# Decode attention on one core: heads 1 to 14 as a loop on the chip over standing buffers

## The chip, the cores and the metric

The kernel runs on one core of a Trainium2 chip. The core has five engines that run their own instruction streams and wait for one another by semaphores: TensorE (PE in the profile; its weight loads are listed as PEld), VectorE (DVE), ScalarE (ACT), GpSimd (POOL) and SyncE (SP). Sixteen DMA engines move data between HBM and the core's memory SBUF; a DMA is issued by an engine's queue, here nearly always SP's. TensorE writes its results to PSUM. The metric is the device time of one execution in microseconds; lower is better. The time before is 1314.99 us, the median of 3 runs (1314.83 to 1315.04).

## What is computed

One decode step of a transformer block in float32: a batch of 2, one new token each of width 448, attention with 16 heads of width 256 over a cache of 8192 keys and values, then a gated feed-forward part.

```python
B, Sq, D = 2, 1, 448
H, Sk, Dh = 16, 8192, 256
def _A_ref(x, k_cache, v_cache, wq, wo):
    q = (x @ wq).reshape(B, Sq, H, Dh).transpose(0, 2, 1, 3)
    scores = jnp.einsum("bhqd,bhkd->bhqk", q, k_cache) * (Dh ** -0.5)
    p = _softmax(scores, axis=-1)
    o = jnp.einsum("bhqk,bhkd->bhqd", p, v_cache)
    return o.transpose(0, 2, 1, 3).reshape(B, Sq, H * Dh) @ wo
h = x + _A_ref(_layernorm(x), k_cache, v_cache, wq, wo)
g, u = _layernorm(h) @ w_gate, _layernorm(h) @ w_up
h2 = h + (g * u) @ w_down
```

The two caches are 268 MB each, so nearly all that is read is cache, and each byte of it is used once.

## The kernel before

The program is written out in full by Python loops; the chip runs it straight through, without a branch.

**Steps.** The work goes in 32 steps, `n = 2 * head + batch`, and a 33rd that finishes (line 306). In step n the scores of (head, batch) number n are formed, and the values of number n - 1 are mixed. A step loads two key tiles and two value tiles, each 128 partitions x 32 keys x 256 numbers, 32 KB on each partition and 4096 KB in all. The order on SP's queue is k0(n), v0(n - 1), k1(n), v1(n - 1) (`load_cache`, line 160). Behind the first v stands a weight tile in three of four steps: `wo` for one head (448 KB, lines 316 to 319) or `wq` for a pair of heads (896 KB, line 320).

**Buffers.** All cache tiles come from one pool, `ring`, with 4 buffers that are handed out in turn. A tile's load waits until the tile four loads earlier has been used up. In the first step only two tiles are loaded, so the second step's k0 and v0 get the third and the fourth buffer. The feed-forward weights (lines 346 to 360) go through the same ring behind the last value tile. The small tiles (scores `s`, `p`, `m`, `rl`, `o_sb` and so on) come from pools of 2.

**One step on the engines.** `scores` (line 232) runs on DVE, in four parts per step: a product of half a key tile with the query, broadcast over the keys (line 239, into the one buffer `prod`), and the sum over the 256 numbers of a key (line 242). A key tile is free for its next load when the product of its second half is done. `top` (line 246) takes the maximum on DVE and transposes it on PE; `softmax` (line 253) is called in the next step behind the first part of the scores: maximum on DVE (line 255), a broadcast on PE (line 257), the exponential on ACT (line 262), the row sum on PE (line 266). `norm` (line 268) takes the reciprocal on DVE behind the second part. `mix` (line 272) multiplies p with a value tile on PE, and `mixed` (line 283) folds the result and, behind batch 1, multiplies it with `wo` into `acc_ps`, which adds up over all heads.

**Queries.** `first_queries` (line 191) and `queries` (line 206) compute q for two heads and both batches at a time on PE; for pair hp + 1 they stand between the two halves of `mix` in the last step of pair hp (line 336). ACT copies them to SBUF.

**The end.** Behind the last step `h_sb` is x plus `acc_ps` (line 389), then come the norm, the gate, the up and the down projections and the output.

The program is laid down in the order in which it is written (`manual_schedule`); each engine runs its own instructions in that order, and waits are put in by the framework where one tile is used by several engines.

Of the kernel before, what the change touches and what calls it, by code (L numbers as in the profile page):

```python
# [24 lines left out]
RING = 4  # L25
WQ, WO = 3 * 2 * DH + DH, 2 * D
# [17 lines left out]
def tile_decode_block(  # L44
# [27 lines left out]
    ps_q = ctx.enter_context(tc.tile_pool(name="ps_q", bufs=2, space=bass.MemoryType.PSUM))  # L72
    ps_s = ctx.enter_context(tc.tile_pool(name="ps_s", bufs=2, space=bass.MemoryType.PSUM))
    ps_1 = ctx.enter_context(tc.tile_pool(name="ps_1", bufs=1, space=bass.MemoryType.PSUM))
# [24 lines left out]
    o_ps = [ps_1.tile([P, 2 * DH], F32, name=f"o_ps{i}") for i in range(2)]  # L99
    for t in o_ps:  # L100
        nc.vector.memset(t, 0.0)  # L101
    acc_ps = ps_1.tile([B, D], F32, name="acc_ps")
    y_ps = ps_1.tile([P, YW], F32, name="y_ps")
    nc.vector.memset(y_ps, 0.0)

# [11 lines left out]
    def center(h, tag):  # L117

        mean = ps_s.tile([P, B], F32, tag="sm", name=f"mean_{tag}")
# [18 lines left out]
    def transposed(src, tag):  # L138
        ps = ps_s.tile([P, DC, B], F32, tag="sm", name=f"T_ps_{tag}")
# [7 lines left out]
    def load_wq(hp):  # L147
        t = wpool.tile([P, WQ], F32, tag="wq", name=f"wq_{hp}")
        nc.sync.dma_start(t, wq[hp])
        return t  # L150

    wo_t = {}

    def load_wo(h):

        if h % 2 == 0:
            wo_t[h // 2] = wpool.tile([P, 2, WO], F32, tag="wo", name=f"wo_{h // 2}")
        nc.sync.dma_start(wo_t[h // 2][:, h % 2, :], wo[h])

    def load_cache(src, b, h, c, name, parts=(JC,)):  # L160
        t = ring.tile([P, JC, DH], F32, tag="ring", name=f"{name}_{h}_{b}_{c}")
        n = P * JC
        keys = src[b, h, c * n : (c + 1) * n].rearrange("(p j) d -> p j d", p=P)
        at = 0
        for k in parts:
            nc.sync.dma_start(t[:, at : at + k, :], keys[:, at : at + k, :])
            at += k
        return t

    w_now = load_wq(0)  # L170
# [6 lines left out]
    var = ps_s.tile([P, B], F32, tag="sm", name="var_x")  # L177
# [13 lines left out]
    def first_queries(w):  # L191

        got = [qpool.tile([P, 2, DH], F32, tag="q", name=f"q_0_{b}") for b in range(B)]
        for k in range(2):
            for b in range(B):
                ps = ps_q.tile([P, DH], F32, tag="q", name=f"q_ps_0_{k}_{b}")
                for c in range(DC):
                    at = c * 2 * DH + (k * DH if c < DC - 1 else 0)
                    nc.tensor.matmul(  # L199
                        ps, xb[:, c + (k if c == DC - 1 else 0), b, :], w[:, at : at + DH],  # L200
                        start=(c == 0), stop=(c == DC - 1),
                    )
                nc.scalar.activation(got[b][:, k, :], ps, AF.Copy)
        return got

    def queries(hp, w):

        got = []
        for b in range(B):
            ps = ps_q.tile([P, 2 * DH], F32, tag="q", name=f"q_ps_{hp}_{b}")  # L210
            for c in range(DC - 1):
                nc.tensor.matmul(  # L212
                    ps, xb[:, c, b, :], w[:, c * 2 * DH : (c + 1) * 2 * DH],
                    start=(c == 0), stop=False,
                )
            for k in range(2):
                nc.tensor.matmul(  # L217
                    ps[:, k * DH : (k + 1) * DH], xb[:, DC - 1 + k, b, :],
                    w[:, 3 * 2 * DH : WQ], start=False, stop=(k == 1),
                )  # L220
            q = qpool.tile([P, 2, DH], F32, tag="q", name=f"q_{hp}_{b}")
            nc.scalar.activation(q.rearrange("p h d -> p (h d)"), ps, AF.Copy)  # L222
            got.append(q)
        return got


    NQ = H * B
    w_t, q_t = {0: w_now}, {0: first_queries(w_now)}
    s_t, p_t, rl_t, l_t, mT_t, oT_t = {}, {}, {}, {}, {}, {}
    HC = JC // 2  # L230

    def scores(i, kt, part):

        h, b = divmod(i, B)
        if part == 0:
            s_t[i] = work.tile([P, NJ], F32, tag="s", name=f"s_{i}")
        c, k = divmod(part, 2)
        q = q_t[h // 2][b][:, h % 2, :]
        nc.vector.tensor_mul(  # L239
            prod, kt[c][:, k * HC : (k + 1) * HC, :], q[:, None, :].to_broadcast([P, HC, DH])  # L240
        )
        nc.vector.tensor_reduce(  # L242
            s_t[i][:, part * HC : (part + 1) * HC], prod, axis=AX.X, op=ALU.add
        )

    def top(i):

        m = work.tile([P, 1], F32, tag="m", name=f"m_{i}")
        nc.vector.tensor_reduce(m, s_t[i], axis=AX.X, op=ALU.max)  # L249
        mT_t[i] = ps_s.tile([1, P], F32, tag="sm", name=f"mT_{i}")  # L250
        nc.tensor.transpose(mT_t[i], m, ident)  # L251

    def softmax(i):
        nm = work.tile([1, 1], F32, tag="nm", name=f"nm_{i}")
        nc.vector.tensor_reduce(nm, mT_t[i], axis=AX.X, op=ALU.max, negate=True)  # L255
        nb_ps = ps_s.tile([P, 1], F32, tag="sm", name=f"nb_ps_{i}")
        nc.tensor.matmul(nb_ps, row, nm, start=True, stop=True)  # L257
        nb = work.tile([P, 1], F32, tag="nb", name=f"nb_{i}")
        nc.scalar.activation(nb, nb_ps, AF.Copy)  # L259
        p_t[i] = work.tile([P, NJ], F32, tag="p", name=f"p_{i}")  # L260
        lsum = work.tile([P, 1], F32, tag="lsum", name=f"lsum_{i}")
        nc.scalar.activation(  # L262
            p_t[i], s_t[i], AF.Exp, bias=nb, scale=DH**-0.5, accum_out=lsum
        )
        l_t[i] = ps_s.tile([P, 1], F32, tag="sm", name=f"l_ps_{i}")
        nc.tensor.matmul(l_t[i], ones, lsum, start=True, stop=True)  # L266

    def norm(i):
        rl_t[i] = work.tile([P, 1], F32, tag="rl", name=f"rl_{i}")
        nc.vector.reciprocal(rl_t[i], l_t[i])  # L270

    def mix(i, vt, c):

        o, p = o_ps[i % 2], p_t[i]
        for t in range(c * JC // 2, (c + 1) * JC // 2):
# [3 lines left out]
                o[g : g + 2, :], p[:, 2 * t : 2 * t + 2], vt[c][:, j : j + 2, :],  # L279
# [3 lines left out]
    def mixed(i):  # L283

        h, b = divmod(i, B)
        o_sb = work.tile([P, 2 * DH], F32, tag="o_sb", name=f"o_sb_{i}")
        nc.scalar.activation(o_sb, o_ps[i % 2], AF.Copy)  # L287
        oT_ps = ps_s.tile([P, 2], F32, tag="sm", name=f"oT_ps_{i}")
# [6 lines left out]
        if b == 0:  # L295
            oT_t[h] = work.tile([P, 2, B], F32, tag="oT", name=f"oT_{h}")
        nc.scalar.activation(oT_t[h][:, :, b], oT_ps, AF.Copy, scale=rl_t[i])  # L297
        if b == B - 1:
            w = wo_t[h // 2][:, h % 2, :]
            for c in range(2):  # L300
                nc.tensor.matmul(  # L301
                    acc_ps, oT_t[h][:, c, :], w[:, c * D : (c + 1) * D],
                    start=(h == 0 and c == 0), stop=(h == H - 1 and c == 1),
                )

    for n in range(NQ + 1):
        kt, vt = [], []
        hp, at = divmod(n, 2 * B)
        for c in range(NCH):
            if n < NQ:  # L310
                parts = FIRST if n == 0 and c == 0 else (JC,)
                kt.append(load_cache(k_cache, n % B, n // B, c, "k", parts))
            if n > 0:
                parts = LAST if n == NQ and c == NCH - 1 else (JC,)
                vt.append(load_cache(v_cache, (n - 1) % B, (n - 1) // B, c, "v", parts))
            if c == 0 and at == 1:
                load_wo(2 * hp)
            if c == 0 and at == 3 and hp + 1 < H // 2:
                load_wo(2 * hp + 1)
            if c == 0 and at == 2 and hp + 1 < H // 2:  # L320
                w_t[hp + 1] = load_wq(hp + 1)
        if n == NQ:
            load_wo(H - 1)
        if n < NQ:
            scores(n, kt, 0)
        if n > 0:
            softmax(n - 1)
# [175 lines left out]
```

## Time and profile before

| what | value |
|---|---|
| median of 3 runs | 1314.99 us |
| the profiled execution's own time | 1314.9 us |
| its span, first to last instruction | 1313.1 us |
| read from HBM | 561.19 MB, 427 GB/s over the span |
| mean granted TensorE clock | 0.653 |
| instructions | 6974 |

The page gives the busy time of each engine, then the span in 40 slices with a digit for the busy share in tenths, then the DMA queues and the largest groups of instructions. A row of a group is: line, engine, operation, written <- read, shapes, count, then busy time and mean time of one in ns, then idle time ahead of it and what ended it. A row of the timeline is: start in us, length in us, engine, line, operation, and in brackets the idle time ahead of it with the engine and line that ended it. A row of DMA issues ends with the size of one in KB and the median time in us from issue to landing. The two operations on which DVE spends nearly all its time, a product and a sum over half a key tile, have these rows:

```profile
L239 DVE TENSOR_TENSOR prod<-k,q 128x4096 f32<-128x4096 f32 x128 | 565.7, 4420 | 115.6 <-DMA k<-in_A_k_cache_dram 110.7
L242 DVE TENSOR_REDUCE s<-prod 128x16 f32<-128x4096 f32 x128 | 565.8, 4420 | 6.0
```

### The profile page before, as it was taken

The numbers are of one execution on the slowest core, as the hardware profiler recorded it, in microseconds if no ns is written. First come the engines' busy times: TensorE is split into PE (matmuls) and PEld (weight loads), VectorE is DVE, ScalarE is ACT, GpSimd is POOL, SyncE is SP. The second block draws the span as 40 slices with busy tenths as digits, with TensorE's granted clock in tenths as the row PEclk, the third lists the DMA queues.
The fourth block names the chain that finished last, engine by engine and source line by source line (L and its number), as shares of the span: only waits on it lengthen the run. The fifth ranks groups of instructions, "written<-read, shape, count | busy, mean of one in ns | idle before, by whom it ended". The sixth has DMA issues, their size and how long they took to land.

```text
span 1313.1 us, 6974 instructions
## 1 busy us (share of the span) xinstructions
PE 569.9 (43%) x2936; PEld 173.4 (13%) x2936; DVE 1153.3 (88%) x395; ACT 60.7 (5%) x183; POOL 1.2 (0%) x8
## 2 busy tenths in 40 slices
PE   3224553354432743426433453524525246254357
PEld 2011110111010210102110021101101002011013
DVE  7999999898998899888998889988998989989971
ACT  1000000000000000000000000000000000000000
POOL 0000000000000000000000000000000000000000
PEclk8556766657765666657666567666676667565668
DMA  9999999999999999999999999999999999999997
GB/s 408 430 430 433 430 432 429 428 433 433 431 428 434 430 431 426 435 429 432 431 431 431 434 429 431 430 425 434 430 431 431 433 428 435 431 430 431 431 424 336
DMA packets 23091, 561.64 MB, mean 428 GB/s; under 512 B 2578, under 2 KB 2580, under 8 KB 5908
## 3 DMA queue, kind: packets, MB, share of 16 engines
q1 hardware_dynamic: 23048, 561.20, 99.6%
q8 instruction: 23, 0.38, 0.1%
q14 instruction: 8, 0.07, 0.0%
q10 hardware_dynamic: 12, 0.01, 0.0%
HBM read 561.19 MB, written 0.00 MB: 427 GB/s over the span
## 4 chain that ended last, share of the span: by engine, by line
DMA 79%; PE 14%; DVE 5%; issue 1%; ACT 0%; POOLq 0%; SPq 0%; POOL 0%
DMA v<-in_A_v_cache_dram 77%; PE o_ps L278 13%; DVE prod L239 3%; DMA wu_t<-in_B_w_up_dram 2%; DVE s L242 2%; PE q_ps L199 0%; PE u_ps L379 0%; PE y_ps L438 0%; DVE o_ps L101 0%; PE hm_ps L431 0%; PE oT_ps L291 0%; ACT o_sb L287 0%; PE mean_x L120 0%; DVE xb L134 0%; PE var_x L178 0%
## 5 line engine op out<-in xcount | busy, mean ns | idle before, releaser
L239 DVE TENSOR_TENSOR prod<-k,q 128x4096 f32<-128x4096 f32 x128 | 565.7, 4420 | 115.6 <-DMA k<-in_A_k_cache_dram 110.7
L242 DVE TENSOR_REDUCE s<-prod 128x16 f32<-128x4096 f32 x128 | 565.8, 4420 | 6.0
L278 PE MATMUL o_ps<-v,p 128*2 128x512 f32 x2048 | 371.3, 891 | 338.1 <-DMA v<-in_A_v_cache_dram 338.1
L278 PEld LDWEIGHTS o_ps<-v,p 128*2 128x2 f32 x2048 | 59.2, 109 | 613.6 <-DMA v<-in_A_v_cache_dram 367.3
L257 PE MATMUL nb_ps<-nm,row 1*128 1x1 f32 x64 | 17.9, 347 | 280.0 <-DVE nm L255 280.0
L257 PEld LDWEIGHTS nb_ps<-nm,row 1*128 1x128 f32 x64 | 15.7, 303 | 287.2 <-issue 158.7
L287 ACT ACTIVATE o_sb<-o_ps 128x512 f32<-128x512 f32 x32 | 19.1, 597 | 679.2 <-PE o_ps L278 679.2
L301 PE MATMUL acc_ps<-wo,oT 128*2 128x448 f32 x64 | 43.9, 834 | 5.6 <-ACT oT L297 5.6
L291 PE MATMUL oT_ps<-sel,o_sb 128*128 128x1 f32 x256 | 33.7, 253 | 23.2 <-ACT o_sb L287 23.2
L212 PE MATMUL q_ps<-wq,xb 128*128 128x512 f32 x84 | 39.1, 601 | 0.0
L291 PEld LDWEIGHTS oT_ps<-sel,o_sb 128*128 128x128 f32 x256 | 31.0, 191 | 55.9 <-ACT o_sb L287 55.9
L251 PE MATMUL mT<-ident,m 128*1 128x128 f32 x32 | 10.2, 318 | 61.2 <-DVE m L249 60.9
L266 PE MATMUL l_ps<-lsum,ones 128*128 128x1 f32 x64 | 18.7, 362 | 23.5 <-ACT p L262 23.5
L259 ACT ACTIVATE nb<-nb_ps 128x1 f32<-128x1 f32 x32 | 5.5, 171 | 406.8 <-PE nb_ps L257 406.8
L266 PEld LDWEIGHTS l_ps<-lsum,ones 128*128 128x128 f32 x64 | 16.0, 310 | 26.2 <-ACT p L262 26.2
L212 PEld LDWEIGHTS q_ps<-wq,xb 128*128 128x128 f32 x84 | 15.4, 190 | 20.6 <-issue 20.3
L217 PE MATMUL q_ps<-wq,xb 128*128 128x256 f32 x56 | 14.4, 379 | 0.0
L251 PEld LDWEIGHTS mT<-ident,m 128*1 128x1 f32 x32 | 2.5, 79 | 84.7 <-issue 50.0
L389 DVE TENSOR_TENSOR h_sb<-x_sb,acc_ps 2x448 f32<-2x448 f32 x1 | 0.6, 609 | 13.8 <-PE acc_ps L301 13.8
L222 ACT ACTIVATE q<-q_ps 128x512 f32<-128x512 f32 x14 | 8.4, 597 | 92.1 <-PE q_ps L217 92.1
L217 PEld LDWEIGHTS q_ps<-wq,xb 128*128 128x128 f32 x56 | 10.6, 190 | 7.4 <-issue 6.7
L262 ACT ACTIVATE p<-s,nb 128x64 f32<-128x64 f32 x32 | 11.1, 348 | 1.0
(79 smaller groups left out, 101.8 us busy)
## 6 DMA issues: line engine op xcount, KB each, us to landing
k<-in_A_k_cache_dram SPq DMA_DIRECT2D x63, 4096.0 KB, 26.5
v<-in_A_v_cache_dram SPq DMA_DIRECT2D x63, 4096.0 KB, 33.2
wq<-in_wq_dram SPq DMA_DIRECT2D x8, 896.0 KB, 34.6
wo<-in_wo_dram SPq DMA_DIRECT2D x16, 448.0 KB, 33.5
k<-in_A_k_cache_dram SPq DMA_DIRECT2D x2, 2048.0 KB, 13.5
wg_t<-in_B_w_gate_dram SPq DMA_DIRECT2D x1, 3136.0 KB, 24.5
wu_t<-in_B_w_up_dram SPq DMA_DIRECT2D x1, 3136.0 KB, 30.4
v<-in_A_v_cache_dram SPq DMA_DIRECT2D x1, 2048.0 KB
```

What stands on the lines that cost most here:

```text
L212: nc.tensor.matmul(ps, xb[:, c, b, :], w[:, c * 2 * DH : (c + 1) * 2 * DH], start=(c == 0), stop=False,)
L217: nc.tensor.matmul(ps[:, k * DH : (k + 1) * DH], xb[:, DC - 1 + k, b, :], w[:, 3 * 2 * DH : WQ], start=False, stop=(k == 1),)
L239: nc.vector.tensor_mul(prod, kt[c][:, k * HC : (k + 1) * HC, :], q[:, None, :].to_broadcast([P, HC, DH]))
L242: nc.vector.tensor_reduce(s_t[i][:, part * HC : (part + 1) * HC], prod, axis=AX.X, op=ALU.add)
L251: nc.tensor.transpose(mT_t[i], m, ident)
L257: nc.tensor.matmul(nb_ps, row, nm, start=True, stop=True)
L262: nc.scalar.activation(p_t[i], s_t[i], AF.Exp, bias=nb, scale=DH**-0.5, accum_out=lsum)
L266: nc.tensor.matmul(l_t[i], ones, lsum, start=True, stop=True)
L278: nc.tensor.matmul(o[g : g + 2, :], p[:, 2 * t : 2 * t + 2], vt[c][:, j : j + 2, :], start=(t < 4), stop=(t >= NJ // 2 - 4),)
L287: nc.scalar.activation(o_sb, o_ps[i % 2], AF.Copy)
L291: nc.tensor.matmul(oT_ps[:, c : c + 1], o_sb[:, (2 * k + c) * P : (2 * k + c + 1) * P], sel[:, k : k + 1], start=(k == 0), stop=(k == 1),)
L301: nc.tensor.matmul(acc_ps, oT_t[h][:, c, :], w[:, c * D : (c + 1) * D], start=(h == 0 and c == 0), stop=(h == H - 1 and c == 1),)
```

## The change

Head 0 and head 15 stay written out; heads 1 to 14 become the body of a loop that the chip runs 14 times, with the head's number in a register (`For_i`). The loop's semaphores are not reset between turns: they only rise, and a wait in the body compares with a register that is stepped in each turn. No engine gets a hint of the branch at the loop's end (`HINT = ()`); PE's body is placed at the start of a block of instructions (`head_align_engines`).

A loop's body needs fixed addresses, so the pools go: there are two key buffers, two value buffers, one `wq`, one `wo`, two `q`, two `s`, two `p`, and one each of `m`, `nm`, `nb`, `lsum`, `rl`, `o_sb` and `oT`. Two PSUM banks `sm_ps` take the small products in separate columns. Weights come head by head: `wq` for head h + 1 in step (h, 1), `wo` of head h - 1 in step (h, 0), and the queries of both batches are formed for one head at a time; ACT takes the second of them behind the last part of the scores. x is added into `acc_ps` by a product with the identity ahead of everything, and `h_sb` becomes a copy. At the end the feed-forward weights go to k0, k1 and v0. The bytes read from HBM stay the same.

```diff
-RING = 4
-WQ, WO = 3 * 2 * DH + DH, 2 * D
+HD = DH // 2
+HINT = ()
+WQ, WO = 3 * DH + DH // 2, 2 * D
...
-    ring = ctx.enter_context(tc.tile_pool(name="ring", bufs=RING))
-    wpool = ctx.enter_context(tc.tile_pool(name="wpool", bufs=2))
-    qpool = ctx.enter_context(tc.tile_pool(name="qpool", bufs=4))
-    work = ctx.enter_context(tc.tile_pool(name="work", bufs=2))
...
+    q_ps = [psum.tile([P, 2 * DH], F32, name=f"q_ps{b}") for b in range(B)]
+    sm_ps = [psum.tile([P, 2 * DH], F32, name=f"sm_ps{i}") for i in range(2)]
+    k_sb = [const.tile([P, JC, DH], F32, name=f"k_sb{c}") for c in range(NCH)]
+    v_sb = [const.tile([P, JC, DH], F32, name=f"v_sb{c}") for c in range(NCH)]
+    wq_sb = const.tile([P, WQ], F32, name="wq_sb")
+    wo_sb = const.tile([P, WO], F32, name="wo_sb")
+    q_sb = [const.tile([P, DH], F32, name=f"q_sb{b}") for b in range(B)]
+    s_sb = [const.tile([P, NJ], F32, name=f"s_sb{b}") for b in range(B)]
+    p_sb = [const.tile([P, NJ], F32, name=f"p_sb{b}") for b in range(B)]
...
+    def load_cache(dst, src, b, h, c, parts=(JC,)):
         n = P * JC
-        keys = src[b, h, c * n : (c + 1) * n].rearrange("(p j) d -> p j d", p=P)
+        keys = src[b, bass.ds(h, 1), c * n : (c + 1) * n].rearrange("o (p j) d -> p (o j) d", p=P)
...
+    nc.tensor.matmul(acc_ps, ident[:B, :B], x_sb[:, :D], start=True, stop=False)
...
+    def query(b):
+        for c in range(DC - 1):
+            nc.tensor.matmul(
+                q_ps[b][:, :DH], xb[:, c, b, :], wq_sb[:, c * DH : (c + 1) * DH],
+                start=(c == 0), stop=False,
+            )
         for k in range(2):
+            nc.tensor.matmul(
+                q_ps[b][:, k * HD : (k + 1) * HD], xb[:, DC - 1 + k, b, :], wq_sb[:, 3 * DH :],
+                start=False, stop=(k == 1),
+            )
+    def take_query(b):
+        nc.scalar.activation(q_sb[b], q_ps[b][:, :DH], AF.Copy)
...
+    def query_steps(h, first, more):
+        for b in range(B):
+            before = b > 0 or not first
+            for c in range(NCH):
+                load_cache(k_sb[c], k_cache, b, h, c, FIRST if first and b == c == 0 else (JC,))
+                if before:
+                    load_cache(v_sb[c], v_cache, 1 - b, h if b else h - 1, c)
+                if c == 0 and b == 0 and before:
+                    load_w(wo_sb, wo, h - 1)
+                if c == 0 and b == 1 and more:
+                    load_w(wq_sb, wq, h + 1)
+            scores(b, 0)
+            if before:
+                softmax(1 - b)
+            scores(b, 1)
+            if before:
+                norm()
             for part in range(2, 2 * NCH):
+                scores(b, part)
+            for c in range(NCH):
+                if c > 0 and b == 1 and more:
+                    query(0)
+                    query(1)
+                    take_query(0)
+                if before:
+                    mix(1 - b, c)
+            if before:
+                mixed(1 - b)
+            top(b)
+            if b == 1 and more:
+                take_query(1)
+
+    for b in range(B):
+        query(b)
+        take_query(b)
+    query_steps(0, True, True)
+    with tc.For_i(1, H - 1, 1, name="heads", iteration_sync="reg_based",
+                  hint_engines=HINT, head_align_engines=(mybir.EngineType.PE,)) as i:
+        query_steps(i, False, True)
+    query_steps(H - 1, False, False)
+    for c in range(NCH):
+        load_cache(v_sb[c], v_cache, B - 1, H - 1, c, LAST if c == NCH - 1 else (JC,))
+    load_w(wo_sb, wo, H - 1)
+    softmax(1)
+    norm()
+    for c in range(NCH):
+        mix(1, c)
+    mixed(1, last=True)
...
+    wg_t = load_ff(k_sb[0], wg)
+    wu_t = load_ff(k_sb[1], wu)
...
-    nc.vector.tensor_add(h_sb[:, :D], x_sb[:, :D], acc_ps)
-    nc.vector.tensor_add(h_sb[:, D:], x_sb[:, D:], acc_ps[:, D - HALF :])
+    nc.vector.tensor_copy(h_sb[:, :D], acc_ps)
+    nc.vector.tensor_copy(h_sb[:, D:], acc_ps[:, D - HALF :])
```

More of the change, by code (lines that the diff above doesn't have):

```diff
@@ L176, in tile_decode_block @@
     xc = center(xT, "x")
-    var = ps_s.tile([P, B], F32, tag="sm", name="var_x")
+    var = sm_ps[0][:, :B]
     nc.tensor.matmul(var, avg, squares(xc, "x"), start=True, stop=True)
@@ L206, in queries @@
[L206 to L224, printed above, removed]
@@ L244, in scores, with top @@
         )
[L246 to L261, printed above, removed]
+    def top(b):
+        nc.vector.tensor_reduce(m_sb, s_sb[b], axis=AX.X, op=ALU.max)
+        nc.tensor.transpose(sm_ps[0][:1, :P], m_sb, ident)
@@ L262, in softmax @@
+    def softmax(b):
+        nc.vector.tensor_reduce(nm_sb, sm_ps[0][:1, :P], axis=AX.X, op=ALU.max, negate=True)
+        nb_ps = sm_ps[1][:, 0:1]
+        nc.tensor.matmul(nb_ps, row, nm_sb, start=True, stop=True)
+        nc.scalar.activation(nb_sb, nb_ps, AF.Copy)
         nc.scalar.activation(
-            p_t[i], s_t[i], AF.Exp, bias=nb, scale=DH**-0.5, accum_out=lsum
+            p_sb[b], s_sb[b], AF.Exp, bias=nb_sb, scale=DH**-0.5, accum_out=lsum_sb
         )
-        l_t[i] = ps_s.tile([P, 1], F32, tag="sm", name=f"l_ps_{i}")
@@ L266, in softmax, with norm, mix @@
[L266 to L274, printed above, removed]
+        nc.tensor.matmul(sm_ps[1][:, 1:2], ones, lsum_sb, start=True, stop=True)
+    def norm():
+        nc.vector.reciprocal(rl_sb, sm_ps[1][:, 1:2])
+    def mix(b, c):
         for t in range(c * JC // 2, (c + 1) * JC // 2):
@@ L278, in mix, with mixed @@
             nc.tensor.matmul(
-                o[g : g + 2, :], p[:, 2 * t : 2 * t + 2], vt[c][:, j : j + 2, :],
+                o_ps[b][g : g + 2, :], p_sb[b][:, 2 * t : 2 * t + 2], v_sb[c][:, j : j + 2, :],
                 start=(t < 4), stop=(t >= NJ // 2 - 4),
             )
[L283 to L288, printed above, removed]
+    def mixed(b, last=False):
+        nc.scalar.activation(o_sb, o_ps[b], AF.Copy)
+        oT_ps = sm_ps[1][:, 2:4]
         for c in range(2):
@@ L306, in tile_decode_block @@
[L306 to L327, printed above, removed]
-        if n < NQ:
-            scores(n, kt, 1)
-        if n > 0:
-            norm(n - 1)
-        if n < NQ:
-            for part in range(2, 2 * NCH):
-                scores(n, kt, part)
-        for c in range(NCH):
-            if c > 0 and at == 3 and hp + 1 < H // 2:
-                q_t[hp + 1] = queries(hp + 1, w_t[hp + 1])
-            if n > 0:
-                mix(n - 1, vt, c)
-        if n > 0:
-            mixed(n - 1)
-        if n < NQ:
-            top(n)
@@ L346, in load_ff @@
-    def load_ff(w, name):
-        t = ring.tile([P, NF * D], F32, tag="ring", name=name)
+                    acc_ps, oT_sb[:, c, :], wo_sb[:, c * D : (c + 1) * D],
+                    start=False, stop=(last and c == 1),
+                )
+    def query_steps(h, first, more):
[15 more added lines that the diff above has]
+                norm()
+            for part in range(2, 2 * NCH):
+                scores(b, part)
[11 more added lines that the diff above has]
+                take_query(1)
@@ L456, in pack @@
     wq, wo = np.asarray(inputs["A_wq"]), np.asarray(inputs["A_wo"])
-    n = 2 * DH
     rows = []
-    for hp in range(H // 2):
-        a = wq[:, hp * n : (hp + 1) * n]
-        top = a[: 3 * P].reshape(3, P, n).transpose(1, 0, 2).reshape(P, 3 * n)
-        last = np.concatenate([a[3 * P :, :DH], a[3 * P :, DH:]], axis=0)
+    for h in range(H):
+        a = wq[:, h * DH : (h + 1) * DH]
+        top = a[: 3 * P].reshape(3, P, DH).transpose(1, 0, 2).reshape(P, 3 * DH)
+        last = np.concatenate([a[3 * P :, :HD], a[3 * P :, HD:]], axis=0)
         rows.append(np.concatenate([top, last], axis=1))
```

93 lines of the change are left out of this document (32 added, 61 removed).

## The prediction

> **What bounds the kernel now.** I read the page first: busy shares, the slices, the DMA queues.
>
> ```profile
> span 1313.1 us, 6974 instructions
> PE 569.9 (43%) x2936; PEld 173.4 (13%) x2936; DVE 1153.3 (88%) x395; ACT 60.7 (5%) x183; POOL 1.2 (0%) x8
> DMA  9999999999999999999999999999999999999997
> GB/s 408 430 430 433 430 432 429 428 433 433 431 428 434 430 431 426 435 429 432 431 431 431 434 429 431 430 425 434 430 431 431 433 428 435 431 430 431 431 424 336
> q1 hardware_dynamic: 23048, 561.20, 99.6%
> k<-in_A_k_cache_dram SPq DMA_DIRECT2D x63, 4096.0 KB, 26.5
> v<-in_A_v_cache_dram SPq DMA_DIRECT2D x63, 4096.0 KB, 33.2
> ```
>
> The 16 DMA engines are busy in every slice, at about 431 GB/s, and only the first and the last slices fall short. All of the 561.20 MB goes through one queue, which SP fills. So the end moves when this queue runs dry, and by as much; nothing else counts unless it makes the queue run dry. VectorE (DVE) is second at 88%. Then the view of waits: how close is DVE behind the stream?
>
> ```profile
> DVE prod L239 <- DMA k<-in_A_k_cache_dram: 110.7, 57, 3.7
> SPq L166 <- DVE prod L239: 858.3, 63, 17.6
> ```
>
> DVE waits for k 110.7 us in 32 steps, 3.5 us a step, 7 us a head. SP in turn waits mostly for DVE to give a k buffer back. Third, one step from the timeline, step 29 (head 14, batch 1), the last that the loop will hold; it gives the rhythm.
>
> ```profile
> 1178.68 4.43 DVE L239 TENSOR_TENSOR prod<-k,q 128x4096 f32<-128x4096 f32 x1 [2.56 <-DMA k<-in_A_k_cache_dram]
> 1188.35 6.53 PE L278 MATMUL o_ps<-v,p 128*2 128x512 f32 x32 [13.31 <-DMA v<-in_A_v_cache_dram]
> ...
> 1196.51 0.22 DVE L249 TENSOR_REDUCE m<-s 128x1 f32<-128x64 f32 x1
> ...
> 1196.79 0.27 PE L251 MATMUL mT<-ident,m 128*1 128x128 f32 x1
> 1198.04 4.42 DVE L239 TENSOR_TENSOR prod<-k,q 128x4096 f32<-128x4096 f32 x1 [1.31 <-DMA k<-in_A_k_cache_dram]
> ```
>
> The second v tile lands at 1188.3, the next k tile at 1198.0: 9.7 us for 4.194 MB, 431 GB/s again. DVE needs 18 us for a k tile, so it ends the step (1196.7) 8 us after the step's last tile has landed. That lag is harmless only because SP has queued the next tile long before: 26.5 us from issue to landing, of which the tile's own 9.7 and about 2.5 of fixed time (below) leave a lead of 14 us.
>
> **The start: two buffers are no longer free (+4.0 us).** The ring of four gave the first step's two k tiles and the second step's k0 and v0 four different slots, so SP issued all at once. With standing buffers k0 of the second step goes into the buffer that the first step still reads, and v0 stands behind it on SP.
>
> ```profile
> 0.73 0.39 SPq L149 DMA_DIRECT2D wq<-in_wq_dram  x1
> 5.37 0.56 PE L178 MATMUL var_x<-sum_sq_x,avg 128*128 128x2 f32 x2 [0.94 <-DVE sum_sq_x L112]
> 7.28 10.12 PE L199 MATMUL q_ps<-wq,xb 128*128 128x256 f32 x32 [1.35 <-DVE xb L134]
> 11.51 4.42 DVE L239 TENSOR_TENSOR prod<-k,q 128x4096 f32<-128x4096 f32 x1 [3.77 <-ACT q L203]
> 24.87 0.33 SPq L166 DMA_DIRECT2D k<-in_A_k_cache_dram  x1
> 42.70 0.33 SPq L166 DMA_DIRECT2D v<-in_A_v_cache_dram  x1
> 60.71 0.33 SPq L166 DMA_DIRECT2D k<-in_A_k_cache_dram  x1
> 64.86 3.62 PE L278 MATMUL o_ps<-v,p 128*2 128x512 f32 x32 [1.64 <-DMA v<-in_A_v_cache_dram]
> L301 PE MATMUL acc_ps<-wo,oT 128*2 128x448 f32 x64 | 43.9, 834 | 5.6 <-ACT oT L297 5.6
> ```
>
> At 64.8 six cache tiles, wq (0.918 MB) and wo (0.459) had landed: 26.54 MB, 61.6 us at 431 GB/s, so landing = 3.2 us + bytes/rate, and 3.2 less the first issue at 0.73 is the 2.5 us of fixed time. In the changed kernel wq is one head, 0.459 MB; with no gap the third k tile would land at 3.2 + 13.04/0.431 = 33.5. But it waits for DVE's second prod, which in this trace freed the buffer at 24.87. The new first product into acc_ps (x_sb through ident) stands on PE ahead of the queries: two instructions of 448 columns at 834 ns, 1.7 us, of which PE's pause from 5.93 to 7.28 hides 1.35; the first query needs as many columns as before, so DVE starts 0.3 to 0.4 later. Issue at 25.3, landing at 25.3 + 2.5 + 9.7 = 37.5: the queue is dry for **4.0 us**. The fourth wait (42.70, now 43.1) comes before k0, v0 and wq have flowed (46.8), so there is no second gap.
>
> **Entering and leaving the loop (+19 and +12 us).** This the trace cannot show, since there is no loop in it, and the diff names no cost. A wait against a register that is stepped each turn needs semaphores with a known count ahead of the first turn, and they must be given back behind the last. I take it that the engines settle once at each edge: SP does not issue the first tile behind the edge until the engines have done everything ahead of it. Below, the cost is nothing, if the constants of head 0 are waited for inside the body and nothing is given back; above, the whole lag of the engines.
>
> ```profile
> 78.54 0.33 SPq L166 DMA_DIRECT2D k<-in_A_k_cache_dram  x1
> ...
> 83.00 0.22 DVE L249 TENSOR_REDUCE m<-s 128x1 f32<-128x64 f32 x1
> ...
> 83.28 0.37 PE L251 MATMUL mT<-ident,m 128*1 128x128 f32 x1 [13.04 <-DVE m L249]
> ```
>
> Entry: DVE is far behind here. Step 1's last transpose ends at 83.65 + 0.4 = 84.0; the next k0 is issued at 84.5 (half a microsecond for the exchange, an estimate from the 0.33 of an issue) and lands at 84.5 + 12.2 = 96.7. Undisturbed, v1 would land at 64.8 + 4.0 - 1.1 (0.459 MB fewer so far) = 67.7 and k0 at 77.5. Dry: **19.2 us**. If only the last prod were waited for (78.54), 14. Exit: the last transpose of step 29 ends at 1197.1; issue at 1197.6, landing at 1209.8 instead of 1198.0: **11.8 us**. Between the ends I take the upper ones, as each wait has one obvious form, "everything before is done"; both ends stay for the range.
>
> **What stays hidden in each turn.** The branch, the steps of the registers, and waits on registers: 14 turns. No row shows a branch, so below is nothing (it can gain nothing, since the stream sets the pace), above is what a turn can hide. DVE: 7 us of waiting for k a head. SP: the lead of 14 us. PE: its last instruction in a turn is the transpose of m; DVE asks for the row sum only behind two products and two reductions.
>
> ```profile
> 636.82 0.27 PE L251 MATMUL mT<-ident,m 128*1 128x128 f32 x1 [1.74 <-DVE m L249]
> ...
> 647.36 0.55 PE L257 MATMUL nb_ps<-nm,row 1*128 1x1 f32 x2 [10.27 <-DVE nm L255]
> ...
> 655.92 0.16 DVE L270 RECIPROCAL rl<-l_ps 128x1 f32<-128x1 f32 x1
> q8 instruction: 23, 0.38, 0.1%
> q14 instruction: 8, 0.07, 0.0%
> ```
>
> PE is idle 10.27 us there in any case. Instructions come in packets of 16 KB (0.38 MB in 23); 0.1% of 16 engines over the span is 21 us, 0.9 us a packet. A few of these on PE, and one on DVE, stay under the cover. Above, a packet could wait behind the tiles, up to the 26.5 us of a k tile. I take 0, the packets being the nearest row. If a turn cost DVE more than 7 us, the excess would count 14 times.
>
> [...]
>
> **Other edits, at nothing.**
>
> ```profile
> L278 PE MATMUL o_ps<-v,p 128*2 128x512 f32 x2048 | 371.3, 891 | 338.1 <-DMA v<-in_A_v_cache_dram 338.1
> ...
> L212 PEld LDWEIGHTS q_ps<-wq,xb 128*128 128x128 f32 x84 | 15.4, 190 | 20.6 <-issue 20.3
> ...
> L217 PEld LDWEIGHTS q_ps<-wq,xb 128*128 128x128 f32 x56 | 10.6, 190 | 7.4 <-issue 6.7
> ```
>
> Queries head by head: PE loads weights twice as often (15.4 + 10.6 us of PEld in the whole run, twice that afterwards), beside 338.1 us in which PE waits for v. Single buffers for m, nm, nb, lsum, rl, o_sb and oT: each is last read in the step that writes it or at the head of the next, and written again a whole step (39 us) later. q_sb[1] is written behind the last product of its step, one turn ahead of its use. At the end h_sb is a copy in place of an addition, same size. The second v tile of the last step now follows the step before's in one buffer:
>
> ```profile
> 1266.05 5.24 PE L278 MATMUL o_ps<-v,p 128*2 128x512 f32 x32 [12.36 <-DMA v<-in_A_v_cache_dram]
> ```
>
> It can be issued at 1271.3, and its first bytes are due when the tile ahead has landed, at 1266.0 + 9.7 = 1275.7; 2.5 us of fixed time leave 1.9 spare. If mix ran 2 us slower there, each further microsecond would count.
>
> **Sum.** 4.0 + 19.2 + 11.8 = 35.0 on the profiled execution's 1314.9 (span 1313.1 and 1.8 around it), which is the median of the runs, 1314.99, to 0.1: **1350 us**.
>
> **Rivals.**
> (a) Only one edge settles: 4 + 11.8 = 1331, or 4 + 19.2 = 1338. For it: at the entry semaphores that start at zero could be raised ahead by constants while SP goes on. Against: nothing in the trace.
> (b) No edge settles: the start alone, 1319. For it: SP is 14 us ahead everywhere in the middle, so a short exchange is free.
> (c) Every turn costs: the excess over DVE's 7 us, or over SP's 14, times 14. With a fetch of 10 us on DVE, between the 0.9 of a packet and the 26.5 of a tile behind the queue, it is 3 x 14 = 42 on top: 1392; a whole settling each turn (11.8 x 14) gives 1480. Against: the change says that nothing is reset in a turn. [...]
> (d) Not slower: the stream flows faster. The slices range from 424 to 435 GB/s; with smaller weights and one fixed set of buffers, 435 throughout would take 561.20/0.435 = 1290 us instead of 1302 at 431, and with no settling the time would be 1307. It decides from 432.4 GB/s, where 4 us are won back. Against: 38 slices scatter about 431 whatever they carry. [...]
> (e) The loop is unrolled or does not overlap heads: then instructions as before, and (b)'s time.
>
> **How the numbers follow.** Both edges 50%: 1344 (entry by the last prod) to 1358 (3 us more at each exchange). (a) 26%, (b) and (e) 14%, (c) 7%, (d) 3%. The range takes in the first three: 1318 to 1358. A measurement tells about 0.2% (2.6 us) from no change: faster 2%, same 5% (parts of b and d at 1312.4 to 1317.6), slower 93%.
>
> **What would show it.** In the slices GB/s should fall in the first, in the third and again near the 37th, and nowhere between. Start: SP's third k issue near 25.3. Entry: SP idle until DVE's second m. Exit: all tiles of head 15's first step issued together. Wrong if SP issues the first k of head 1 near 61 (no settling there), if the k waits of DVE disappear (DVE bound, case c), or if the slices between fall below 428.

## The result, and the profile after

The changed kernel takes 1347.89 us, the median of 6 runs (1347.25 to 1348.19); the kernel before takes 1315.03 us beside it. The ratio is 1.0249, 95% interval 1.0236 to 1.0263: slower by 33 us. The forecast was 1350.

The page of the changed kernel, in the rows shown of before:

```profile
span 1346.1 us, 8485 instructions
PE 548.9 (41%) x3086; PEld 190.9 (14%) x3086; DVE 1153.6 (86%) x395; ACT 61.5 (5%) x197; POOL 1.3 (0%) x8
DMA  8959999999999999999999999999999999978998
GB/s 357 419 211 426 433 434 430 430 428 434 432 429 427 433 428 437 429 429 434 431 429 429 434 434 427 430 429 436 429 429 428 434 433 424 434 342 356 433 423 350
q1 hardware_dynamic: 24200, 561.20, 97.3%
q8 instruction: 7, 0.11, 0.0%
q14 instruction: 3, 0.02, 0.0%
```

The same bytes flow, and DVE is busy for the same 1153 us. The queue ran dry in the first slice, in the third, and again where the 36th and the 37th meet; between them the rate is that of before. The view by windows sizes the three dips; in each row the window and its length come first, the DMA share and GB/s last.

```profile
20.00:30.00 10.00, 0.00 (x0) 0.00 (x0) 9.90 (x4) 0.00 (x0) 0.00 (x0) 0.50 0.67 262
...
66.00:88.00 22.00, 5.97 (x48) 2.47 (x46) 17.20 (x5) 1.24 (x3) 0.00 (x0) 0.70 0.19 71
...
1200.00:1220.00 20.00, 7.31 (x41) 1.99 (x41) 14.93 (x5) 1.13 (x3) 0.00 (x0) 0.61 0.37 146
```

Against the steady 431 GB/s the first dip loses 10 x (1 - 262/431) = 3.9 us, the second 22 x (1 - 71/431) = 18.4, the third 20 x (1 - 146/431) = 13.2: 35.5 us in all. What SP waited for there stands in its own waits (waiter and line, engine and line it waited for; total, times, longest). Line 308 is the loop statement, line 167 a cache load.

```profile
SPq L167 <- DVEq L308: 38.4, 1, 38.4
SPq L308 <- DMA v_sb<-in_A_v_cache_dram: 33.2, 1, 33.2
...
SPq L308 <- DVE m_sb L227: 8.4, 1, 8.4
...
SPq L308 <- PE sm_ps L228: 0.4, 1, 0.4
```

At the entry SP is not stopped: it goes into the loop, and the first k load of the body waits for an entry that DVE makes at the loop statement, at 83.1 us, behind all that DVE has of head 0. At the exit SP waits, still at the loop statement, for the last v tile to land, then for DVE's last maximum, then for PE's last transpose. In the timeline (start, length, what; in brackets the idle time ahead and its end):

```profile
67.49 3.62 PE L248 MATMUL o_ps<-v_sb,p_sb 128*2 128x512 f32 x32 [0.56 <-DMA v_sb<-in_A_v_cache_dram]
...
83.11 0.22 DVE L227 TENSOR_REDUCE m_sb<-s_sb 128x1 f32<-128x64 f32 x1
83.35 0.35 SPq L167 DMA_DIRECT2D k_sb<-in_A_k_cache_dram  x1
...
96.93 4.42 DVE L218 TENSOR_TENSOR prod<-k_sb,q_sb 128x4096 f32<-128x4096 f32 x1 [13.60 <-DMA k_sb<-in_A_k_cache_dram]
...
1206.67 5.88 PE L248 MATMUL o_ps<-v_sb,p_sb 128*2 128x512 f32 x32 [10.23 <-DMA v_sb<-in_A_v_cache_dram]
...
1215.12 0.37 PE L228 MATMUL sm_ps<-ident,m_sb 128*1 128x128 f32 x1 [0.71 <-DVE m_sb L227]
1216.10 0.34 SPq L167 DMA_DIRECT2D k_sb<-in_A_k_cache_dram  x1
...
1228.40 4.43 DVE L218 TENSOR_TENSOR prod<-k_sb,q_sb 128x4096 f32<-128x4096 f32 x1 [13.33 <-DMA k_sb<-in_A_k_cache_dram]
```

Counted by landings, as the prediction did it: ahead of the entry the last v tile lands at 67.4, so the next k tile was due 9.7 us later at 77.2; it lands at 96.9 (forecast 96.7), 19.7 us late. At the exit the last v tile lands at 1206.6, the next k tile was due at 1216.4 and lands at 1228.4, 12.0 us late. The windows, which count bytes and not finished tiles, put 1.3 us less on the one and 1.2 more on the other; the sum is the same.

Three dips make 35.5 us, yet the span grew by 33.0. Between step 5 and step 29 the changed kernel was quicker; these are the first products of the two steps, before and after:

```profile
195.90 4.43 DVE L239 TENSOR_TENSOR prod<-k,q 128x4096 f32<-128x4096 f32 x1 [1.40 <-DMA k<-in_A_k_cache_dram]
...
1158.12 4.43 DVE L239 TENSOR_TENSOR prod<-k,q 128x4096 f32<-128x4096 f32 x1 [1.38 <-DMA k<-in_A_k_cache_dram]
```

```profile
216.87 4.43 DVE L218 TENSOR_TENSOR prod<-k_sb,q_sb 128x4096 f32<-128x4096 f32 x1 [1.31 <-DMA k_sb<-in_A_k_cache_dram]
...
1176.47 4.42 DVE L218 TENSOR_TENSOR prod<-k_sb,q_sb 128x4096 f32<-128x4096 f32 x1 [1.31 <-DMA k_sb<-in_A_k_cache_dram]
```

962.2 us before, 959.6 after, for the same bytes: 2.6 us won in the loop. 35.5 - 2.6 = 32.9.

### The profile page after: what moved, and what is told of

It reads as the page before. It is cut to its first block, busy times and chain, and to the rows that moved or that the text cites. A ratio compares the mean times of both kernels' runs of the same rounds, so it can differ in the third digit from the quotient of the medians.

```text
span 1346.1 us, 8485 instructions
## 1 busy us (share of the span) xinstructions
PE 548.9 (41%) x3086; PEld 190.9 (14%) x3086; DVE 1153.6 (86%) x395; ACT 61.5 (5%) x197; POOL 1.3 (0%) x8
## 5 line engine op out<-in xcount | busy, mean ns | idle before, releaser
L218 DVE TENSOR_TENSOR prod<-k_sb,q_sb 128x4096 f32<-128x4096 f32 x128 | 565.7, 4420 | 147.9 <-DMA k_sb<-in_A_k_cache_dram 142.8
L221 DVE TENSOR_REDUCE s_sb<-prod 128x16 f32<-128x4096 f32 x128 | 565.8, 4420 | 5.4
L248 PE MATMUL o_ps<-v_sb,p_sb 128*2 128x512 f32 x2048 | 357.5, 861 | 353.0 <-DMA v_sb<-in_A_v_cache_dram 353.0
L248 PEld LDWEIGHTS o_ps<-v_sb,p_sb 128*2 128x2 f32 x2048 | 57.6, 107 | 611.2 <-DMA v_sb<-in_A_v_cache_dram 372.8
L202 PE MATMUL q_ps<-wq_sb,xb 128*128 128x256 f32 x192 | 50.8, 403 | 0.0
L259 PE MATMUL sm_ps<-sel,o_sb 128*128 128x1 f32 x256 | 33.7, 253 | 26.3 <-ACT o_sb L255 26.3
L259 PEld LDWEIGHTS sm_ps<-sel,o_sb 128*128 128x128 f32 x256 | 31.0, 191 | 56.9 <-ACT o_sb L255 56.9
L202 PEld LDWEIGHTS q_ps<-wq_sb,xb 128*128 128x128 f32 x192 | 35.6, 199 | 18.8 <-issue 13.5
L266 PE MATMUL acc_ps<-wo_sb,oT_sb 128*2 128x448 f32 x64 | 34.7, 678 | 5.6 <-ACT oT_sb L263 5.6
L238 PE MATMUL sm_ps<-lsum_sb,ones 128*128 128x1 f32 x64 | 18.8, 362 | 25.1 <-ACT p_sb L235 25.1
L207 PEld LDWEIGHTS q_ps<-wq_sb,xb 128*128 128x128 f32 x128 | 19.9, 196 | 1.8
L207 PE MATMUL q_ps<-wq_sb,xb 128*128 128x128 f32 x128 | 19.9, 279 | 0.0
L213 ACT ACTIVATE q_sb<-q_ps 128x256 f32<-128x256 f32 x32 | 12.2, 380 | 134.1 <-PE q_ps L207 128.6
```

The lines of the kernel that those rows point to most:

```text
L202: nc.tensor.matmul(q_ps[b][:, :DH], xb[:, c, b, :], wq_sb[:, c * DH : (c + 1) * DH], start=(c == 0), stop=False,)
L207: nc.tensor.matmul(q_ps[b][:, k * HD : (k + 1) * HD], xb[:, DC - 1 + k, b, :], wq_sb[:, 3 * DH :], start=False, stop=(k == 1),)
L213: nc.scalar.activation(q_sb[b], q_ps[b][:, :DH], AF.Copy)
L218: nc.vector.tensor_mul(prod, k_sb[c][:, k * HC : (k + 1) * HC, :], q_sb[b][:, None, :].to_broadcast([P, HC, DH]))
L221: nc.vector.tensor_reduce(s_sb[b][:, part * HC : (part + 1) * HC], prod, axis=AX.X, op=ALU.add)
L238: nc.tensor.matmul(sm_ps[1][:, 1:2], ones, lsum_sb, start=True, stop=True)
```

## The experiments

The theory: SP's queue runs dry at the start because two buffers are no longer free, and at the two edges of the loop because SP waits there for engines that lag behind the stream; the turns are free. The rivals: the standing buffers and the weights head by head cost more than the start; an edge has a fixed price; the turns cost. All times below stand beside a kernel before of 1315.0 to 1315.15 us.

### The change without its loop

```diff
-    with tc.For_i(1, H - 1, 1, name="heads", iteration_sync="reg_based",
-                  hint_engines=HINT, head_align_engines=(mybir.EngineType.PE,)) as i:
+    for i in range(1, H - 1):
         query_steps(i, False, True)
```

> Everything of the change but the loop: heads 1 to 14 written out over the same standing buffers. Theory (the loop costs only at its two edges, where SP waits for the other engines, and the standing buffers cost only the dry queue at the start): 1315.0 + 3.9 = 1319, less up to 2.6 us that the stream of the changed kernel won in the middle; so 1316.5 to 1319, with one dip of GB/s in the first slice and none later. Rival (standing and single buffers or weights head by head cost more than the start): above 1325. Rival (the turns of the loop cost, not its edges): the same 1319, so this run doesn't tell that one apart.

1319.32 us (ratio 1.0033, interval 1.0021 to 1.0045). Its slices have one dip, the first:

```profile
GB/s 361 431 427 428 433 434 429 430 428 431 431 433 429 432 429 430 431 429 434 429 430 431 432 429 430 432 426 433 431 429 431 431 431 432 431 427 429 434 420 343
```

That is 0.3 us above the expected range. So 28.6 of the 33 us belong to the loop, and 4.3 to everything else in the change. The 2.6 us of the middle are not there without the loop (962.6 us between the same two products): the buffers and the weights did not win them.

### Without the loop, the free loads first

```diff
+            early = first and b == 1
             for c in range(NCH):
+                if early:
+                    load_cache(v_sb[c], v_cache, 1 - b, h, c)
+                    if c == 0:
+                        load_w(wq_sb, wq, h + 1)
+                    else:
+                        load_cache(k_sb[c], k_cache, b, h, c)
+                        continue
                 load_cache(k_sb[c], k_cache, b, h, c, FIRST if first and b == c == 0 else (JC,))
...
```

> As the first, and in the second step SP issues v0, wq, k0, v1, k1 in place of k0, v0, wq, k1, v1, so that the loads that wait for nothing flow while k0 waits for DVE. Theory: the dry 3.9 us of the start are gone: 1312.5 to 1315, level with the kernel before or up to 0.2% faster. Rival (the first dip is DVE's late start and not the order of the loads): no change from the first run.

1316.69 us, the median of 11 runs that scatter more than the others (1315.57 to 1318.1); ratio 1.0014, interval 1.0005 to 1.0023. The trace is of the quickest of them. In the window that lost 3.9 us it moves 419 GB/s in place of 262:

```profile
20.00:30.00 10.00, 0.00 (x0) 0.00 (x0) 9.90 (x4) 0.00 (x0) 0.00 (x0) 0.50 0.97 419
```

The dip is a matter of the order of the loads, as expected. The time fell by 2.6 us and not by 3.9, and stayed a little above the range; why it scatters is open.

### With the loop, the free loads first

The same edit in the changed kernel.

> The changed kernel with the loop, and the second step's loads in the order v0, wq, k0, v1, k1. Theory: at the loop's entry SP waits for DVE's end of step 1 at 83.3 us, wherever the queue stands, so filling the queue earlier only moves the dry time from the start to the entry: 1347.9 +- 1. Rival (start and entry are two separate losses that add, 3.9 + 18.4): 1344.

1348.36 us (1347.68 to 1348.68), no gain. In the slices the first is full again (408 in place of 357), and the second is lower by as much (368 in place of 419):

```profile
GB/s 408 368 208 429 433 434 431 428 430 434 432 429 428 433 427 437 429 430 434 431 428 430 434 432 428 431 430 434 430 429 430 434 430 426 433 344 355 431 424 352
```

The end of the dry time at the entry is set by DVE's end at 83.3 us; a queue that was fuller before only runs dry for longer. So the first two terms add up in a sum, but taking the first away alone gives nothing back.

### The loop from head 4

```diff
-    with tc.For_i(1, H - 1, 1, name="heads", iteration_sync="reg_based",
+    for i in range(1, 4):
+        query_steps(i, False, True)
+    with tc.For_i(4, H - 1, 1, name="heads", iteration_sync="reg_based",
```

> Heads 1 to 3 written out too, the loop runs over 4 to 14. Theory (an edge costs the lag of DVE behind the stream): at the end of head 3 DVE is some 8 us behind the last tile as everywhere in the middle, no longer 16: the entry costs 11 to 13 in place of 18.4 and the time falls to 1341 to 1343. Rival (an edge has a fixed price): 1348. Rival (each turn costs): lower by three turns of 14 of what the loop costs, at 31 us 6.6 us, the same number; the place of the dip then tells: theory has one dip near 350 us of the span and none at 66.

1342.12 us. The dip at 66 us is gone and stands at the new entry (between 300 and 325 us, not near 350); it is a smaller one, 25 x (1 - 229/431) = 11.7 us in place of 18.4:

```profile
66.00:88.00 22.00, 6.85 (x53) 3.32 (x51) 21.83 (x7) 1.63 (x4) 0.00 (x0) 0.74 0.99 424
```

```profile
300.00:325.00 25.00, 6.61 (x41) 1.92 (x41) 16.92 (x5) 1.13 (x3) 0.00 (x0) 0.67 0.56 229
```

The entry has no fixed price: it goes with the lag that DVE has there. At this entry DVE ends 8.4 us behind the last landing (308.7 to 317.1), at the one near 66 us it ended 15.9 behind (67.4 to 83.3), and the dip is 6.7 us smaller.

### Two loops behind one another

```diff
-    with tc.For_i(1, H - 1, 1, name="heads", iteration_sync="reg_based",
+    with tc.For_i(1, 8, 1, name="heads", iteration_sync="reg_based",
...
+    with tc.For_i(8, H - 1, 1, name="heads2", iteration_sync="reg_based",
+                  hint_engines=HINT, head_align_engines=(mybir.EngineType.PE,)) as i:
+        query_steps(i, False, True)
```

> Two loops, over heads 1 to 7 and 8 to 14, straight after one another: one more exit and one more entry, the same turns. Theory (at an exit SP waits until the landed tiles are used up, 13.2 us of dry queue; at the entry right behind it DVE has nothing left to finish, so the entry adds next to nothing): 1347.9 + 13 to 14.5 = 1361 to 1362.5, with one new dip near 670 us of the span. Rival (an exit and an entry each cost what they cost in the changed kernel, 13.2 + 18.4): 1379.

1362.4 us: 14.5 more, for an exit and an entry together. The one new dip stands in the 19th and 20th slices (612 to 680 us):

```profile
GB/s 360 407 217 436 430 431 432 432 429 433 430 431 430 433 431 428 436 433 407 267 435 432 431 432 430 430 432 430 430 433 431 432 432 432 433 357 337 431 425 353
```

Of the 14.5 the exit takes some 13.2, as in the changed kernel; that leaves 1.3 us for the entry behind it.

### Two turns in place of fourteen

```diff
-    with tc.For_i(1, H - 1, 1, name="heads", iteration_sync="reg_based",
+    with tc.For_i(1, 3, 1, name="heads", iteration_sync="reg_based",
...
+    for i in range(3, H - 1):
+        query_steps(i, False, True)
```

> The loop runs over heads 1 and 2 only; heads 3 to 14 are written out. The two edges stay, 12 of the 14 turns go. Theory (turns cost nothing): the exit dip moves to about 250 us of the span, and the time is 1348 to 1351: not shorter, and up to 3 us longer, since the programs written out so far each show two or three jumps of 1.4 us in the spacing of the steps that the loop doesn't show. Rival (each turn costs a branch with a fetch, some 1 to 2 us): 1324 to 1336.

1351.14 us, at the top of the range: 3.3 us more than with 14 turns. A turn costs nothing that can be seen; a head written out costs 0.3 us more than a turn (3.3 by 12). In the trace of before a packet of 16 KB took 1.0 to 1.3 us, and PE's longest branch in the changed kernel took 0.36: by that estimate the rival's turn is 1.4 to 1.7 us, twelve of them 16 to 20, and none of it is seen.

### Hints at the branches

```diff
-HINT = ()
+HINT = None
```

> The changed kernel with a branch hint on every engine in place of none. Theory: branches are off the stream's path and the slowest in the trace takes 0.36 us, so 1347.9 +- 0.8. [...]

1347.74 us against 1347.89: no difference. In the changed kernel, without hints, the branches at the loop statement are short (ns: least, median, most):

```profile
L308 SPq COMPARE_BRANCH  x15: 40/45/54, 44.6 to 1172.7; - x15
L308 ACTq COMPARE_BRANCH  x15: 40/45/50, 79.0 to 1214.8; - x15
L308 DVEq COMPARE_BRANCH  x15: 50/56/67, 83.6 to 1215.0; - x15
L308 PEldq COMPARE_BRANCH  x15: 76/208/359, 84.0 to 1215.2; - x15
```

### A stop between turns

```diff
-iteration_sync="reg_based"
+iteration_sync="barrier"
```

> The loop with a stop of all engines between turns, in which the semaphores are reset, in place of semaphores that only rise. Theory (a settling costs the lag of DVE behind the stream, 13.2 us at the exit): 13 more of them, each 13 to 15 us, on 1347.9: 1517 to 1543. [...]

1492.83 us, below the range. A turn takes 694.45 - 601.86 = 92.6 us in place of (1197.02 - 1117.07) = 80.0. The rows are the first product on the second k tile of a head's second step, here one turn apart and in the changed kernel again:

```profile
601.86 4.42 DVE L218 TENSOR_TENSOR prod<-k_sb,q_sb 128x4096 f32<-128x4096 f32 x1 [2.62 <-DMA k_sb<-in_A_k_cache_dram]
...
694.45 4.43 DVE L218 TENSOR_TENSOR prod<-k_sb,q_sb 128x4096 f32<-128x4096 f32 x1 [2.63 <-DMA k_sb<-in_A_k_cache_dram]
```

```profile
1117.07 4.43 DVE L218 TENSOR_TENSOR prod<-k_sb,q_sb 128x4096 f32<-128x4096 f32 x1 [2.58 <-DMA k_sb<-in_A_k_cache_dram]
...
1197.02 4.42 DVE L218 TENSOR_TENSOR prod<-k_sb,q_sb 128x4096 f32<-128x4096 f32 x1 [2.56 <-DMA k_sb<-in_A_k_cache_dram]
```

14 settlings of 12.6 us are 177 us; 1319.3 + 177 - 2.6 = 1493.7. What the expectation got wrong is mainly the entry, which costs nothing in this form: the third slice moves 433 GB/s, and step 3 begins at 118.95 us, where the kernel before begins it at 119.05.

```profile
118.95 4.42 DVE L218 TENSOR_TENSOR prod<-k_sb,q_sb 128x4096 f32<-128x4096 f32 x1
```

So the 18.4 us of the entry came with `reg_based`, where semaphores go on rising from turn to turn, and not with the same loop under `barrier`.

### The body turned by half a step

The loop is cut at another place: a turn begins with the second key tile of step (h, 0) and ends behind the first key tile of step (h + 1, 0). `half_1` has the first two parts of the scores with softmax and norm, `half_2` the rest of the step; `loads` keeps each step's order, and the free loads come first at the start.

```diff
...
+    def turn(h, first=False):
+        half_2(0, before=not first)
+        loads(1, h, first)
+        half_1(1)
+        half_2(1)
+        loads(0, h + 1)
+        half_1(0)
...
-    query_steps(0, True, True)
+    loads(0, 0, True)
+    half_1(0, False)
+    turn(0, True)
     with tc.For_i(1, H - 1, 1, name="heads", iteration_sync="reg_based",
                   hint_engines=HINT, head_align_engines=(mybir.EngineType.PE,)) as i:
-        query_steps(i, False, True)
-    query_steps(H - 1, False, False)
+        turn(i)
+    half_2(0)
+    loads(1, H - 1, more=False)
+    half_1(1)
+    half_2(1, more=False)
```

> The same loop of 14 turns with its body turned by half a step: a turn begins with the second key tile of step (h, 0) and ends behind the first key tile of step (h + 1, 0), so that at both edges three of four tiles are loaded or under way while DVE finishes; and the start in the order v0, wq, k0, v1, k1. Theory (an edge costs what the queue is dry while SP waits for the other engines, so its price hangs on where the loop is cut): the entry costs 0 to 1 us; at the exit SP still waits for the last load of the loop to land, 2.5 us of fixed time and the exchange, 3 to 4.5 us; with the 2 to 3 us that a loop gains in the middle: 1316 to 1319. Rival (an edge has a price of its own, whatever the engines do there): 1345 to 1348.

1317.87 us, the median of 10 runs (1316.81 to 1319.61); ratio 1.0021, interval 1.0012 to 1.003. Thirty of the 33 us are back with the loop in place. The order of the loads at the start alone gave nothing there (1348.36 us); the cut alone, without that order, was not run. SP makes the same two waits as in the changed kernel (line 335 is the loop statement here; the trace is of the slowest run, 1319.61 us):

```profile
SPq L335 <- DMA v_sb<-in_A_v_cache_dram: 33.6, 1, 33.6
...
SPq L167 <- DVEq L335: 16.1, 1, 16.1
```

```profile
85.00:105.00 20.00, 7.44 (x36) 2.04 (x36) 19.93 (x7) 0.61 (x3) 0.00 (x0) 0.59 0.99 424
...
1215.00:1240.00 25.00, 11.65 (x76) 2.90 (x76) 13.47 (x4) 0.86 (x2) 0.00 (x0) 0.70 0.81 337
```

At the entry SP waits 16.1 us for DVE while the queue still holds tiles: 20 x (1 - 424/431) = 0.3 us are lost. At the exit 25 x (1 - 337/431) = 5.5 us, a little above the 3 to 4.5 expected: SP waits for the last tile to land, and by then nothing is behind it. It doesn't beat the kernel before; no version here does.

### More instructions, with nothing to do

The version without a loop, and on GpSimd 5120 memsets of one number:

```diff
+    spare = const.tile([1, 1], F32, name="spare")
+    for _ in range(20 * 256):
+        nc.gpsimd.memset(spare, 0.0)
```

> The version without a loop and 5120 small memsets on GpSimd, which nothing waits for: some 20 more packets of instructions in the 1317 us. In the changed kernel 21 packets fewer went with 2 to 3 us less. Theory (instruction packets hold up the data on the DMA engines that carry them): 1319.3 + 2 to 3 = 1321 to 1322.5. Rival (the loop's gain in the middle has another cause): 1319.3 +- 0.5.

1342.09 us: 22.8 more than without them, some ten times the expectation. The packets of instructions are 40 more, not 20 (8 KB each, 0.32 MB more in 40; at the 0.45 MB that 6974 instructions took before, 5120 make 0.33), and all on the second queue:

```profile
GB/s 359 435 427 427 433 431 428 431 430 429 431 431 431 424 425 420 412 407 418 417 410 415 421 416 426 429 427 432 431 429 432 430 429 432 429 432 431 430 325 323
q8 instruction: 24, 0.39, 0.1%
q14 instruction: 48, 0.39, 0.1%
```

Without the memsets these queues have 24 and 8. 22.8 us by 40 packets are 0.57 us each, but they are not paid packet by packet. GpSimd runs the memsets from 1.8 to 753 us and fetches a packet every 18.8 us; up to the 13th slice (436 us) the rate is that of the run without them, then it falls, and the 39th slice is short as well (325 in place of 420).

The trace shows why. It has each load's landing in 16 parts, as many as there are DMA engines. From 49 us on nearly every packet on the second queue sets the part that lands last back by about 0.65 us: it comes 0.9 us behind the first part at 14 us, 7.3 behind at 234 us and 16.6 behind at 483 us. The first part of the load that is complete at 483 us still lands at 466.7 us, as without the memsets. From there the lag stays at 16 to 17.6 us until the memsets end, and the whole stream is slower with it (407 to 425 GB/s in the 14th to the 22nd slice); at the end, from 1290 to 1300 us, it moves 203 GB/s. So the packets hold up the part that lands last, and a load is used only when that part is there: in the changed kernel the last of a k tile's 16 parts lands at 96.81 us, 1.02 behind the 15th, and DVE's product on it starts at 96.93.

### The same work for GpSimd in few instructions

```diff
+    spare = const.tile([P, 2048], F32, name="spare")
+    for _ in range(230):
+        nc.gpsimd.memset(spare, 0.0)
```

> The version without a loop and 230 large memsets on GpSimd (128 x 2048), some 450 us of work for GpSimd as in the run before, but with only 2 more packets of instructions in place of 40. Theory (the 22.8 us of the run before came with its 40 packets, 0.57 us each): 1319.3 + 1 = 1320.5 at most. Rival (GpSimd's own work in SBUF holds up the DMAs): 1335 to 1345.

1322.48 us, 3.2 more than without memsets, outside the range of either side. But 3.1 of them are lost before step 1 begins (its first product stands at 50.46 us against 47.40), and the distance stays about 3 to the end: GpSimd is busy for 416 us in this run and the stream is as quick as without it. The part of a load that lands last comes 5.0 us behind the first at most, against 5.2 without memsets. So it is not GpSimd's work that held up the stream in the run before, but its 40 packets.

## Why the prediction was right

**What bounds it.** Right. Time was lost only where SP's queue ran dry, and DVE's busy time didn't change.

**The start, +4.0.** 3.9 by the windows, 4.3 by the run without the loop. One thing the sum hid: with the loop in place the term can't be taken out by itself, since the entry that follows is set by DVE's end. One figure beside the term does not come out: with `wq` for one head, k0, v0 and wq have flowed at 45.8 us and not at 46.8. The fourth wait still ends ahead of that.

**Entry, +19.2, and exit, +11.8.** 19.7 and 12.0 by landings. The prediction took "the engines settle once at each edge" from the need to start and to hand back semaphores that only rise. The trace has the first: at the loop statement SP adds to eight semaphores at 43.7 to 44.2 us, and ACT, DVE and PE to one each at 78.7, 83.1 and 83.4. The second was its author's assumption and was not shown: behind the last turn SP waits there and adds nothing. The runs show two different things under the name of settling: at the entry SP waits for DVE alone, and at the exit for the last landing, DVE and PE. The entry needn't cost that: the loop with a stop between turns enters for nothing. That both edges wait was a choice between two bounds that no row before the change could settle. The entry's landing, right to 0.2 us, owes something to luck: SP issued at 83.35 us and not at 84.5, as it waited for DVE alone, and the tile then took 13.6 us to land and not 12.2 (its last part came 1.7 us behind the first, 0.6 for the tile before; a packet of instructions had been fetched at 88.9 us). The two errors cancel. And 3 us more at each of two exchanges makes 1356, not the 1358 at the top of the range.

**The turns, 0.** Right; two turns (1351.14), fourteen turns (1347.89) and hints (1347.74) show it. PE's branches take 0.36 us at most. The whole run has 10 packets of instructions, fewer than turns, and none between 153 and 1178 us, where nearly all the turns are.

**Other edits, 0.** Right within 0.3 us: the change without its loop is at 1319.32, where rival (b) stood at 1319.

**What the sum lacked.** 2.6 us won in the middle. The versions written out have 31 or 32 packets of instructions, the loop has 10, none of them between 153 and 1178 us. The landings in parts tell what this is worth. In the kernel before, the last part of a load comes 2.2 us behind the first at step 5 and 5.5 behind at step 29. Nearly all of that comes in two jumps of 1.4 us, right behind the 9th and the 17th packet of 16 KB on the first queue (550 and 1031 us); the packets between leave the last part where it is. Without the loop the lag grows from 2.0 to 5.0 between the two steps; in the loop it stays at 1.7 to 1.8. So the lag grows by 3.0 to 3.3 us less in the loop, which is 2.6 to 3.0 us quicker than these two. The prediction priced a packet at 0.9 us on the engine that fetches it, and hid it there; it left out that a packet holds up a part of the stream.

## What to carry to other kernels

Where a DMA queue sets the pace, price a loop by its edges: at each, ask which engine the issuing queue will wait for, how far that engine is behind the stream, and how much is still queued. Cut a loop where the loads for the next piece are already issued: here that took the entry from 18.4 us to 0.3. Where buffers are fixed, look at the first round: a load that must wait should not stand ahead of loads that need not (2.6 us here, without the loop). And look at the part of a load that lands last: with 40 more packets it came 16 to 17.6 us behind the first, and the run took 22.8 us longer.

## What was not expected of the hardware

Fetching instructions was not free for this stream, which is bound by DMA: 40 packets, 0.32 MB beside 561 MB, cost 22.8 us. The price is hidden for the engine (the 5120 memsets start 0.147 us apart all along, with one gap above 0.2 us) and not for the stream. While GpSimd ran large memsets, three copies on DVE at the start took 6.01 us in place of 1.07, and DVE's products and sums kept their 4.42:

```profile
7.35 6.01 DVE L149 COPY xb<-xn 128x768 f32<-128x768 f32 x3
...
14.66 4.43 DVE L218 TENSOR_TENSOR prod<-k_sb,q_sb 128x4096 f32<-128x4096 f32 x1 [1.30 <-ACT q_sb L213]
```
